# Batch 0's norms pair by pair through Ln and Exp on ScalarE, with its copies and casts moved off ScalarE

## The chip, the cores and the metric

One core of one Trainium2 chip. The metric is the device time of one execution, in microseconds (us), as the median of several. Here "slow" is a run over 1.5% above the fastest of the same kernel. The kernel before has a spread of its own, 475.9 to 483.5 over all its runs (476.21 at a mean clock of 0.999 and 482.3 at 0.987 in one set of rounds), so it is always run beside the kernel that it is compared with. "Clock" is the clock granted to TensorE, the matrix engine, as the profile records it: 1.00 is full speed, 0.50 half.

## The reference

```python
q_n = q / (norm(q, axis=-1) + 1e-6);  k_n likewise          # q, k, v: 8 batches x 12 heads x 448 x 64, fp32
attn = softmax(q_n @ k_n^T / tau)                            # tau = 0.1
x = (attn @ v) laid out as 3584 x 768
h = x @ w_in;  out = (h * sigmoid(1.702 * h)) @ w_out        # 768 -> 2048 -> 768
```

## The kernel before

Two heads make a "pair"; six pairs make a batch. A small planner in the kernel gives each operation an engine, an estimated duration and a due time, and fixes the order on every engine when the program is built. An engine runs its instructions in that order, whatever happens on the chip. Where the plan foresees a gap on TensorE in the first 50 us, it puts filler transposes there, to keep the clock up.

```python
def norm_a(grp):                      # one chain of small VectorE operations for a group of pairs
    ...                               # y = bits of a turned into a first guess of 1/sqrt(a)
    newton(grp, RS_A, RS_B)           # 3 operations
def norm_b(grp):
    newton(grp, 0.5, 1.5)             # 3 operations
    ...                               # y / (y * 1e-6 + 1): add, reciprocal, multiply
groups = [(0,), (1, 2), (3, 4, 5)]    # batch 0: three norms for six pairs

def fill():
    nc.tensor.transpose(out=tps0[:, 2 * S : 2 * S + 128], in_=ident, identity=ident)

# in the plan's emit(): fillers ahead of a TensorE operation that is planned later than TensorE is free
while free < KEEP_WARM and free + FILL_SPARE < now:
    fill()
    free += FILL_US
```

ScalarE squares q and k, VectorE sums, a norm follows, GpSimd scales (VectorE for pair 0's q), TensorE transposes and makes scores, ScalarE takes Exp, TensorE attends. The second part (tanh for the sigmoid) begins with `mm1_h`, line 529 of the kernel before.

## Time and profile before

| | before |
|---|---|
| time, median of 3 (range) | 479.46 us (475.9 to 480.62) |
| span of the profiled run | 479.4 us |
| TensorE busy | 463.7 us, 97% |
| ScalarE busy | 310.0 us, 65% |
| first product of the second part | 42.97 us |
| fillers on TensorE | 326 |

The prediction below shows the lines and reads them. PE is TensorE, PEld its weight loads, DVE VectorE, ACT ScalarE, POOL GpSimd. A line of a timeline gives the start and the time taken in us, engine, line of the kernel, operation, tile written <- tile read with their sizes, how many, and in brackets the wait ahead of it and what ended that. A line of a table of stretches gives the stretch, its length, busy us (and instructions) of the five, the clock, the transfers' share and GB/s. Cuts are marked by "...".

### The profile page before, as it was taken

Reading aid. Unit: us, or ns where it says so; the run is one execution under the profiler, and the core shown is the slowest. Engines: PE = TensorE matmul, PEld = TensorE weight load, DVE = VectorE, ACT = ScalarE, POOL = GpSimd, SP = SyncE. Lnnn points to the kernel's source line nnn. Section 1 sums busy time; section 2 is a strip of 40 time slices with the busy share of each in tenths; the row PEclk is TensorE's granted clock in tenths of the full one; section 3 lists DMA queues with packets and bytes.
Section 4 is the critical chain, followed back from the end, with each engine's and each line's share of the span. In section 5 each row is a group of like instructions: output and inputs, shape, how many; then the busy total and the mean of one; then the engine's idle time right before and its main releaser. Section 6 shows DMA issues by size and latency. Waiting matters only on the chain.

```text
span 479.4 us, 9003 instructions
## 1 busy us (share of the span) xinstructions
PE 463.7 (97%) x3382; PEld 268.0 (56%) x3382; DVE 275.4 (57%) x663; ACT 310.0 (65%) x491; POOL 132.1 (28%) x189
## 2 busy tenths in 40 slices
PE   8889999999999999999999999999999999999996
PEld 8768888664444554445444554445444554555563
DVE  6746887687687736864495735963373315532500
ACT  4669869679887567776777567865666556423411
POOL 1452741656633422406151422415100000000000
PEclk9999999599999999999999999999999999999999
DMA  9999599978965558446564567343310222022022
GB/s 219 238 238 246 89 177 243 261 205 205 231 161 116 140 146 177 115 110 185 145 160 100 140 162 180 95 125 94 89 45 3 62 68 63 2 62 67 1 58 75
DMA packets 81435, 63.50 MB, mean 132 GB/s; under 512 B 40232, under 2 KB 74864, under 8 KB 81392
## 3 DMA queue, kind: packets, MB, share of 16 engines
q1 hardware_dynamic: 77504, 56.41, 47.3%
q0 software_dynamic: 3648, 6.29, 7.3%
q8 instruction: 26, 0.43, 0.4%
q10 hardware_dynamic: 240, 0.23, 0.1%
q14 instruction: 17, 0.14, 0.1%
HBM read 49.81 MB, written 11.14 MB: 127 GB/s over the span
## 4 chain that ended last, share of the span: by engine, by line
PE 75%; DMA 10%; DVE 6%; ACT 4%; SPq 2%; issue 1%; POOL 1%; ACTq 0%
PE mm L554 30%; PE mm L499 22%; PE avp L363 10%; PE sp L344 7%; DMA k<-in_k_dram 4%; DMA w_out<-in_moe_w_out_dram 4%; PE mm L409 2%; ACT expT L355 2%; DVE xT L487 2%; ACT sq L238 1%; DVE n L244 1%; DMA v<-in_v_dram 1%; DMA q<-in_q_dram 1%; DVE gT L516 1%; PE tps L323 1%; SPq L230 1%
## 5 line engine op out<-in xcount | busy, mean ns | idle before, releaser
L355 ACT ACTIVATE expT<-sp 112x896 f16<-112x896 f32 x192 | 166.7, 917 | 57.2 <-PE sp L344 45.9
L554 PE MATMUL mm<-w_out,gT 128*128 128x384 f16 x896 | 155.1, 328 | 0.0
L499 PE MATMUL mm<-xT,w_in 128*128 128x448 f16 x672 | 134.0, 353 | 1.9 <-DVE gT L516 1.9
L554 PEld LDWEIGHTS <-gT 128*128 128x128 f16 x896 | 84.4, 98 | 66.2 <-issue 14.1
L499 PEld LDWEIGHTS <-w_in 128*128 128x128 f16 x672 | 63.2, 98 | 68.5 <-issue 13.5
L516 DVE SCALAR_TENSOR_TENSOR gT<-th,mm 128x448 f16<-128x448 f16 x112 | 67.8, 617 | 56.2 <-ACT th L509 55.7
L509 ACT ACTIVATE th<-mm 128x448 f16<-128x448 f32 x128 | 69.4, 545 | 38.1 <-PE mm L499 31.1
L244 DVE TENSOR_REDUCE n<-sq 112x8 f32<-112x512 f32 x96 | 63.9, 677 | 38.2 <-ACT sq L238 37.7
L307 POOL CAST vt<-v 112x256 f16<-112x256 f32 x84 | 32.3, 402 | 161.9 <-PE avp L363 95.9
L380 DVE TENSOR_SCALAR av<-avp 65x448 f16<-65x448 f32 x72 | 44.4, 617 | 47.2 <-PE avp L363 46.9
L363 PE MATMUL avp<-expT,vt 112*128 112x448 f16 x288 | 66.5, 352 | 0.6 <-DVE av L380 0.6
L295 POOL TENSOR_TENSOR qks<-k,y 112x512 f16<-112x512 f32 x48 | 50.2, 1046 | 56.0 <-DVE y L285 30.9
L565 ACT ACTIVATE ost<-mm 128x384 f32<-128x384 f32 x56 | 27.5, 491 | 44.2 <-PE mm L554 42.6
L295 POOL TENSOR_TENSOR qks<-q,y 112x512 f16<-112x512 f32 x47 | 49.1, 1045 | 6.8 <-DVE xT L487 6.8
L344 PE MATMUL sp<-qkT 64*112 64x448 f16 x288 | 43.0, 372 | 0.0
L363 PEld LDWEIGHTS <-vt 112*128 112x128 f16 x288 | 27.8, 97 | 25.6 <-issue 1.3
L238 ACT ACTIVATE sq<-k 112x512 f32<-112x512 f32 x48 | 30.4, 636 | 14.8 <-DMA k<-in_k_dram 12.9
L487 DVE TENSOR_TENSOR xT<-av,rcb 64x448 f16<-64x448 f16 x72 | 31.3, 434 | 11.8 <-DMA rcb<-rcp 10.8
L238 ACT ACTIVATE sq<-q 112x512 f32<-112x512 f32 x48 | 30.2, 634 | 8.1 <-DMA q<-in_q_dram 5.2
L344 PEld LDWEIGHTS <-qkT 64*112 64x112 f16 x288 | 13.1, 124 | 27.7 <-issue 27.7
L323 PE MATMUL tps<-ident 128*128 128x128 f16 x326 | 23.4, 234 | 4.9 <-DVE qkT L327 3.4
L409 PE MATMUL mm<-vt,expT 112*112 112x65 f16 x384 | 25.7, 222 | 0.5 <-ACT expT L355 0.4
(39 smaller groups left out, 230.3 us busy)
## 6 DMA issues: line engine op xcount, KB each, us to landing
k<-in_k_dram SPq DMA_DIRECT2D x48, 224.0 KB, 3.0
v<-in_v_dram SPq DMA_DIRECT2D x48, 224.0 KB, 3.2
q<-in_q_dram SPq DMA_DIRECT2D x47, 224.0 KB, 4.4
rcb<-rcp SPq DMA_DIRECT2D x24, 168.0 KB, 3.1
w_in<-in_moe_w_in_dram POOLq DMA_DIRECT2D x2, 1536.0 KB, 16.1
w_out<-in_moe_w_out_dram POOLq DMA_DIRECT2D x2, 1536.0 KB, 15.1
out_dram<-ost SPq DMA_DIRECT2D x7, 336.0 KB
out_dram<-ost SPq DMA_DIRECT2D x8, 288.0 KB
```

The costliest lines, as they stand in the source:

```text
L238: return nc.scalar.activation(out=sqs[x, ti], in_=src, func=AF.Square)
L244: nc.vector.tensor_reduce(out=n2s[grp][:, x - grp[0], ti], in_=sqs.pop((x, ti)), axis=AX.X, op=ALU.add,)
L295: return eng.tensor_tensor(out=qkss[x][:, ti].rearrange("p c j d -> p j c d"), in0=src, in1=rss[x][:, ti, :, :, None].to_broadcast((P, 2, ...
L344: nc.tensor.matmul(out=sp[:, j, :S], lhsT=qkT[64 * j : 64 * (j + 1), 1, c * P : (c + 1) * P], rhs=qkT[64 * j : 64 * (j + 1), 0, :], start= ...
L355: nc.scalar.activation(out=e, in_=sps.pop(key)[:, :, :S], func=AF.Exp, scale=inv_tau, **kw)
L363: nc.tensor.matmul(out=ps, lhsT=vts[x % NV][:, c, j], rhs=exps[x, c][:, j], start=(c == 0), stop=(c == C - 1),)
L380: nc.vector.tensor_scalar(out=avs[x][:n, j], in0=ps[:n], scalar1=AV_SCALE, scalar2=None, op0=ALU.mult)
L487: last = nc.vector.tensor_tensor(out=xT[r], in0=av[r, j], in1=rcbs[x // GRP][r, x % GRP], op=ALU.mult)
L499: nc.tensor.matmul(out=ps[:, :S], lhsT=w_in_sb[:, kk, 128 * m : 128 * (m + 1)], rhs=xTs[b, kk], start=(kk == 0), stop=(kk == KT1 - 1),)
L509: nc.scalar.activation(out=ths[key], in_=mms[key][:, :S], func=AF.Tanh, scale=0.851)
L516: nc.vector.scalar_tensor_tensor(out=gts[b // 2][:, m, (b % 2) * S : (b % 2 + 1) * S], in0=ths.pop((b, m)), scalar=1.0, in1=mms.pop((b, m) ...
L554: nc.tensor.matmul(out=mms[b2, t, n][:, :NW], lhsT=gts[b2][:, kk, 128 * t : 128 * (t + 1)], rhs=w_out_sb[:, kk, NW * n : NW * (n + 1)], st ...
```

## The change

The intent: VectorE's Newton chains go. `exp(0.5 * ln(a))` on ScalarE gives the norm, VectorE adds 1e-6 and takes the reciprocal. Each pair of batch 0 has its own norm, so that no pair waits for another's load. To make room on ScalarE, the turned copies go to VectorE and the v casts of pairs 2 to 5 to GpSimd (`XA` and `CA` name the pairs whose copies and casts stay on ScalarE; `SQP`, for squares on GpSimd, is empty).

```diff
+    SQP, SQT, XA, CA = (), (0, 1), (), (0, 1)
...
+    def root(grp):
+        a = n2s[grp]
+        nc.scalar.activation(out=a, in_=a, func=AF.Ln)
+        nc.scalar.activation(out=a, in_=a, func=AF.Exp, scale=0.5)
+
+    def inverse(grp):
+        ...
+        nc.vector.tensor_scalar(out=y, in0=a, scalar1=1e-6, scalar2=None, op0=ALU.add)
+        last = nc.vector.reciprocal(out=y, in_=y)
...
-        copy = nc.scalar.copy if x < HP else nc.gpsimd.tensor_copy
+        copy = nc.scalar.copy if x in CA else nc.gpsimd.tensor_copy
...
-        (nc.scalar.copy if b + h == 0 else nc.vector.tensor_copy)(
+        (nc.scalar.copy if x in XA and not h else nc.vector.tensor_copy)(
...
-    groups = [(0,), (1, 2), (3, 4, 5)]
+    groups = [(x,) for x in range(HP)]
...
+            if first:
+                add(("norm", 0, grp), "ACT", 0.48, early + 0.3, partial(root, grp), after=reds)
+                add(("norm", 1, grp), "DVE", 0.45, early + 0.3, partial(inverse, grp), after=[("norm", 0, grp)])
```

A table load (`ACT_TABLE_LOAD` in the traces) is the instruction that stands on ScalarE wherever it goes over to the functions of another table set.

More of the change, by code (lines that the diff above doesn't have):

```diff
@@ L196 @@
     p_sq = pool("p_sq", 2)
-    p_n = pool("p_n", 2)
+    p_n = pool("p_n", 3)
     p_qks = pool("p_qks", 3)
@@ L233, in load, with sq_pool @@
         )
+    def sq_pool(x, ti):
+        return x in SQP and ti in SQT
     def square(x, ti):
@@ L237, in square @@
         src = (q32, k32)[ti][x]
+        if sq_pool(x, ti):
+            return nc.gpsimd.tensor_tensor(out=sqs[x, ti], in0=src, in1=src, op=ALU.mult)
         return nc.scalar.activation(out=sqs[x, ti], in_=src, func=AF.Square)
@@ L289, in norm_b @@
         return last
+    def root(grp):
[3 more added lines that the diff above has]
+    def inverse(grp):
+        a = n2s.pop(grp)
+        y = p_n.tile([P, len(grp), 2, 2, C], FP32, name=f"yv_{len(grp)}")
+        nc.vector.tensor_scalar(out=y, in0=a, scalar1=1e-6, scalar2=None, op0=ALU.add)
+        last = nc.vector.reciprocal(out=y, in_=y)
+        for x in grp:
+            rss[x] = y[:, x - grp[0]]
+        return last
     def scale(x, ti, eng):
@@ L623 @@
                 takes=[(nm, 1)], dma=PAIR, hold=hold, turn=True)
-            add(("sq", ti, x), "ACT", 0.53, early + ti * 0.1, partial(square, x, ti),
-                after=[("load", nm, x)], takes=[("sq", 1)])
+            pl = sq_pool(x, ti)
+            add(("sq", ti, x), "POOL" if pl else "ACT", 1.0 if pl else 0.53, early + ti * 0.1, partial(square, x, ti),
+                after=[("load", nm, x)], takes=[("sq", 1), ("port", int(pl))], frees=[("port", int(pl))])
             add(("red", ti, x), "DVE", 0.6, early + 0.2, partial(reduce, x, ti),
@@ L634 @@
             n = len(grp)
+            if first:
+                add(("norm", 0, grp), "ACT", 0.48, early + 0.3, partial(root, grp), after=reds)
+                add(("norm", 1, grp), "DVE", 0.45, early + 0.3, partial(inverse, grp), after=[("norm", 0, grp)])
+        if x == grp[0] and not first:
             add(("norm", 0, grp), "DVE", 0.78 + 0.06 * n, early + 0.3, partial(norm_a, grp), after=reds, **port)
@@ L638 @@
             takes=[("v", 1)], dma=PAIR, hold=hold, turn=True)
-        add(("cast", x), "ACT" if first else "POOL", 0.64 if first else 0.75, s - 0.5, partial(cast_v, x),
-            after=[("load", "v", x)], takes=[("vt", 1), ("port", 1 - first)], frees=[("v", 1), ("port", 1 - first)])
+        ca = x in CA
+        add(("cast", x), "ACT" if ca else "POOL", 0.64 if ca else 0.75, s - 0.5, partial(cast_v, x),
+            after=[("load", "v", x)], takes=[("vt", 1), ("port", 1 - ca)], frees=[("v", 1), ("port", 1 - ca)])
         if x < TURN:
@@ L664 @@
                     frees=[("xs", 1)])
-                add(("x", x, h), "ACT" if first and not h else "DVE", 0.35, sh + 1, partial(turned_h, x, h), after=[("turn", x, h)],
+                add(("x", x, h), "ACT" if x in XA and not h else "DVE", 0.35, sh + 1, partial(turned_h, x, h), after=[("turn", x, h)],
                     takes=[("x", 1 - h)], frees=[("mm", 1)])
```

## The prediction

> **What bounds the kernel now.** I read the busy table first, then the forty slices, the table of stretches, the chain of waits, and last the timelines of ScalarE, GpSimd, VectorE and TensorE over the first 60 us, because the change touches batch 0 alone (pairs 0 to 5).
>
> ```profile
> PE 463.7 (97%) x3382; PEld 268.0 (56%) x3382; DVE 275.4 (57%) x663; ACT 310.0 (65%) x491; POOL 132.1 (28%) x189
> ...
> PE   8889999999999999999999999999999999999996
> ...
> ACT  4669869679887567776777567865666556423411
> ...
> PEclk9999999599999999999999999999999999999999
> ...
> PE mm L554 30%; PE mm L499 22%; PE avp L363 10%; PE sp L344 7%; DMA k<-in_k_dram 4%; DMA w_out<-in_moe_w_out_dram 4%; PE mm L409 2%; ACT expT L355 2%; DVE xT L487 2%; ACT sq L238 1%; DVE n L244 1%; DMA v<-in_v_dram 1%; DMA q<-in_q_dram 1%; DVE gT L516 1%; PE tps L323 1%; SPq L230 1%
> ...
> 0.00:10.00 10.00, 8.64 (x109) 8.64 (x110) 6.67 (x39) 3.77 (x6) 1.32 (x7) 1.00 0.88 212
> 10.00:20.00 10.00, 9.21 (x162) 8.73 (x159) 7.67 (x21) 7.43 (x16) 4.42 (x6) 1.00 1.13 247
> 20.00:30.00 10.00, 7.90 (x127) 6.74 (x125) 5.31 (x18) 6.35 (x13) 5.21 (x6) 1.00 1.11 218
> 30.00:40.00 10.00, 8.48 (x128) 6.94 (x127) 3.73 (x10) 7.64 (x12) 2.71 (x3) 1.00 1.12 270
> 40.00:50.00 10.00, 9.78 (x140) 8.63 (x139) 9.09 (x28) 9.94 (x17) 4.54 (x8) 1.00 0.72 180
> ...
> 70.00:100.00 30.00, 27.94 (x300) 22.78 (x298) 21.42 (x57) 22.50 (x36) 10.40 (x18) 0.83 1.02 245
> ...
> 1.36 10.82 PE L323 MATMUL tps<-ident 128*128 128x128 f16 x145 [1.36 <-POOL ident masks.py:199]
> ...
> 42.97 1.32 PE L529 MATMUL mm<-xT,w_in 128*128 128x224 f16 x12
> ...
> 1.19 1.28 ACT L238 ACT_TABLE_LOAD   x1 [1.19 <-PEq L807]
> ...
> 14.66 0.92 ACT L355 ACTIVATE expT<-sp 112x896 f16<-112x896 f32 x1 [2.19 <-PE sp L392]
> ...
> 17.00 0.82 POOL L590 DMA_DIRECT2D w_in<-in_moe_w_in_dram  x1 [2.70 <-DVE y L285]
> ...
> 26.67 1.04 POOL L295 TENSOR_TENSOR qks<-k,y 112x512 f16<-112x512 f32 x1 [4.79 <-DVE y L285]
> ```
>
> See first that TensorE is busy in nearly every slice, so from about 43 us on the span is its work laid end to end. Ahead of that, "busy" deceives: 145 of the first instructions are filler transposes of the identity that keep its clock up. The first useful product of the second part (the 12 matmuls at 42.97) marks when the filling ends. So the start is a latency chain (load, square, sum, norm, scale, transpose, scores, exponential, attend), and a microsecond saved or lost before that mark is a microsecond of span, if the TensorE work behind it is unchanged. ScalarE is far from full at first (3.8 us of the first 10) but 9.9 of 10 between 40 and 50. The granted clock fell to half for part of one slice near 85 us; the whole 70 to 100 stretch has 0.83, which is 5.1 us of full clock lost, about the spread of the three runs (475.9 to 480.62).
>
> The last two lines show what the change aims at. GpSimd stood idle 2.7 and 4.8 us for a Newton result: pairs 1 and 2 share one norm, and so do pairs 3 to 5, so pair 3 cannot be scaled before pair 5 is loaded. Their scales start only at 17.84 and 26.67.
>
> **What the Trainium skill says.** "ScalarE: Activation LUTs", section "What ACT_TABLE_LOAD costs", gives 1283 ns for a table load plus about 1380 ns of drain, 2.66 us for a switch; the same section gives an activation with immediates 186 ns + 0.833 ns an element. The trace agrees with the load (1.28) and the activation (917 ns for 896 elements in the row of exponentials; the formula says 932), but its one load is followed by a wait for a transfer, so it cannot show the drain. "Table sets: the hidden batching unit" on that page says that Exp sits with tanh in one set, and that Ln and Exp together have another set of their own. "ScalarE activation tables: per-element evaluation and per-set limits", section "Table sets in the compiler and the runtime", says that the back end places loads by the longest run. Here the order of the built instructions decides: the kernel before has 1 load, the changed one 13. Every Ln is preceded by a load of another set, and every Exp of a norm by a load of the first set. The shared set is not used. "TensorE: Matmul & The Clock Gate", section "What's actually happening", says that an idle window of about 3.4 us halves the clock; the 5 in the clock row, just after TensorE's waits of 1.25, 0.41 and 0.41 us at 84 us, fits.
>
> **The change part by part.**
> Removed from VectorE: three Newton chains of 10 small operations. Pair 0's runs from 6.44 to 8.57, 2.1 us; that of pairs 1 and 2 from 14.34 to 16.69, 2.3 us; that of pairs 3 to 5 is 2.5 us of operations about a qkT copy. Sum 6.9 us. Added: six times an addition and a reciprocal on 16 columns (0.21 + 0.29 from their start spacing), 3.0 us, and six turned copies at about 0.2, 1.2 us. Net relief about 2.7 us on an engine that is not the bound here.
> Removed from ScalarE: six turned copies at 0.24 spacing, 1.4 us, and four pairs of v casts at 0.6, 2.4 us. Added: six Ln and six Exp on 16 columns, an estimate of 0.2 us each by the page's formula, 2.4 us; and 12 table loads at 1.28, 15.4 us. Net +14 us, before any drain. ScalarE worked 25.2 us in the first 40, so about 39 of 40 is asked of it.
> GpSimd gains the four v casts (0.74 a pair, 3.0 us), lying beside other work. Its first weight load moves behind pair 1's two scales, but pair 1 no longer waits for the second weight load. The fillers ahead of pair 0's transposes drop from 145 to 127, at 75 ns 1.3 us less.
>
> Now the chain, placing the new ScalarE order with the old spacings (square 0.52, exponential 0.82, casts 0.6, load 1.28; the ends of the last one where something depends on it).
> Pair 0: squares as before, done 6.47; load 7.75; Ln 8.0; load 9.3; Exp 9.5. Inverse on VectorE until 10.0, then its scale until 10.7 and GpSimd's until 11.8, against 8.6, 9.3 and 10.4. Nearly free, since the transposes began only at 12.02, behind fillers.
> Pair 1: squares to 10.55, load, Ln, load, Exp: 13.6. The copy of pair 0's transposes stands behind this inverse on VectorE: 14.1 instead of 12.61. Scores at 14.7 instead of 14.22. GpSimd scales pair 1 at 14.1, 3.7 us earlier than before.
> Pair 2: two squares and a v cast to 15.25, norm to 18.3. Only then comes a square and the first softmax exponential, at 18.7 instead of 14.66.
> Pair 3: norm 19.6 to 22.6, then a square and the second exponential at 23.0 instead of 16.51. Both score buffers are held until then, so TensorE waits.
> Pair 4: two squares, a v cast and a square to 25.65, norm to 28.7. Two exponentials, a square, two exponentials: 32.5. Pair 5: norm to 35.5. Inverse 36.1, GpSimd scales to 38.1, transposes, copy, scores: its two exponentials end near 43.2 after those of pairs 3, 4 and 0 again. Attend, normalise, turn: the first product at about 46.0 against 42.97, 3.0 late. Useful TensorE work ahead of it is alike (seven attends, some eight halves of scores in both).
> Each of the 12 switches lies on this serial chain, so 0.1 us of hand-over at each adds 1.2: 4.2 us late. Behind the mark, ScalarE has no squares of batch 1 done where before it had four, so five tanh steps later it needs 8 exponentials, 10 squares and 5 tanh (13.9 us) where the trace took 13.4. Another 0.5 to 2 us lost; I take 1.3. After that ScalarE is some 75% busy and TensorE hides it. TensorE's gaps between 17 and 37 us get longer, two of them near 2.5 us with few fillers between: I allow 1.5 us for a halved clock there. Sum 4.2 + 1.3 + 1.5 = 7.0 us: 486.5 us.
>
> **The rivals.**
> One: the switch costs the page's full 2.66 us. Nothing in the old trace excludes it. For it: the page says so. Against: a drain of about the load's own length could be the sequencer waiting for the same load and not a further cost; the other page gives only 1283 ns between sets. It would add 12 x 1.38 = 16.6 us to the chain, longer clock gaps too: about 500 to 505 us. I give it one in four.
> Two: what the change intends. Loads hide in ScalarE's early idle time and pair-by-pair norms free GpSimd sooner: pairs 3 to 5 start up to 4 us earlier than the old 26.67. For it: ScalarE has 15 idle us in the first 40 and the scales of pair 3 should come at 22.9. Against: the exponentials that pairs 0 and 1 need are queued behind the loads. If a few more of the loads lie in waits than I placed there, 476 to 480 us.
> Three: the half-clock spell of 82 to 92 us does not recur in the new order: up to 5.1 us gained, which would bring my sum back to about 481; or a second one falls on useful work: 491.
>
> **Range and chances.** Between rival two and a mild form of rival one lie 8 chances in 10: 478.5 to 501 us. Faster by over 2% is below 469.9, for which the mark would have to come by 34 us while ScalarE is full: 3%. Slower by over 2% is above 489.05: rival one (25%), half of the cases with an intermediate hand-over (8%), and a bad clock spell (5%): 38%. Within 2%: 59%.
>
> **What would show each step.** Thirteen table loads with the gap behind each to its Ln or Exp: under 0.2 us speaks for my sum, over 1 us for rival one. First exponential at 18 to 20 us; the second over 3.5 us later. First product at 45.5 to 48. ScalarE over 90% in the stretches from 10 to 40. Scales of pairs 1 and 3 at about 14 and 23, earlier than before, yet without gain. The clock row with a new 5 in the first four slices. I am wrong if the loads overlap with waits and the mark comes before 43, or if the span changes by much more than the mark does: then the rest of the order, not ScalarE's start, decides.

## The result

The changed kernel takes 491.95 us (median of 4, 491.48 to 492.33) against 479.55 (the three runs above and one more): a ratio of 1.0273, 95% interval 1.0227 to 1.032, slower. (Ratios here are the mean time of one kernel's fast runs over that of the other's of the same rounds, so not quite the ratio of the medians.)

The changed kernel's page: the busy row, then TensorE, ScalarE and the granted clock in the forty slices.

```profile
PE 471.2 (96%) x3315; PEld 273.3 (56%) x3315; DVE 272.6 (56%) x651; ACT 322.9 (66%) x501; POOL 135.3 (28%) x197
...
PE   8769999999999999999999999999999999999996
...
ACT  7994768699888755876678656784677456423411
...
PEclk9575789999999999999999999999999999999999
```

ScalarE gained 12.9 us of work, and the clock row has changed: five of the first six slices are below 9. Cut along the clock, the table of stretches of the changed kernel says it better.

```profile
13.90:24.20 10.30, 8.76 (x79) 7.64 (x79) 4.55 (x11) 10.18 (x17) 6.67 (x7) 0.50 1.03 195
24.20:31.00 6.80, 4.06 (x70) 3.63 (x69) 3.46 (x10) 6.74 (x12) 2.81 (x4) 1.00 1.11 211
31.00:54.90 23.90, 22.54 (x197) 18.20 (x195) 8.40 (x26) 14.73 (x19) 6.07 (x13) 0.50 0.78 199
...
68.50:72.00 3.50, 3.50 (x26) 2.92 (x25) 1.45 (x5) 1.06 (x2) 3.50 (x8) 0.51 0.21 14
```

From 13.9 to 31 us ScalarE works nearly without a break (10.18 of 10.30, 6.74 of 6.80) and TensorE waits for it (4.06 of 6.80 busy). Then the clock falls to half for 23.9 us, and now TensorE is full, at half speed, and ScalarE waits (14.73 of 23.90).

The changed kernel's ScalarE in order of time, pair 0's norm and the later exponentials:

```profile
5.75 0.63 ACT L244 ACTIVATE sq<-k 112x512 f32<-112x512 f32 x1 [0.23 <-DVE n L250]
6.40 1.28 ACT L300 ACT_TABLE_LOAD   x1
7.70 0.21 ACT L300 ACTIVATE n<-n 112x16 f32<-112x16 f32 x1
7.93 1.28 ACT L301 ACT_TABLE_LOAD   x1
9.22 0.21 ACT L301 ACTIVATE n<-n 112x16 f32<-112x16 f32 x1
9.35 0.61 ACT L244 ACTIVATE sq<-q 112x512 f32<-112x512 f32 x1
...
18.66 0.90 ACT L376 ACTIVATE expT<-sp 112x896 f16<-112x896 f32 x1
...
23.03 0.90 ACT L376 ACTIVATE expT<-sp 112x896 f16<-112x896 f32 x1
...
35.64 0.21 ACT L301 ACTIVATE n<-n 112x16 f32<-112x16 f32 x1
35.77 2.52 ACT L376 ACTIVATE expT<-sp 112x896 f16<-112x896 f32 x3
41.07 1.77 ACT L376 ACTIVATE expT<-sp 112x896 f16<-112x896 f32 x2 [2.79 <-PE sp L413]
```

A norm is load, Ln, load, Exp, 3.0 us, and the step from one to the next costs 0.01 to 0.02 us: there is no drain behind a load. From 4.4 to 38 us nothing on this engine waits long; from then on it does, for scores.

The changed kernel's TensorE where it waited, and where the clock was down:

```profile
29.49 0.40 PE L413 MATMUL sp<-qkT 64*112 64x224 f16 x4 [2.19 <-ACT expT L376]
...
42.33 1.67 PE L430 MATMUL mm<-vt,expT 112*112 112x65 f16 x16
...
51.09 2.45 PE L550 MATMUL mm<-xT,w_in 128*128 128x224 f16 x12
...
55.58 0.98 PE L430 MATMUL mm<-vt,expT 112*112 112x65 f16 x16
```

Sixteen attend matmuls take 1.67 us in the spell and 0.98 after it. The first product of the second part, called the mark from here on, comes at 51.09, 8.1 us later than before.

### The profile page after: what moved, and what is told of

Read it like the earlier page. It is cut to its first block, busy times and chain, and to the rows that moved or that the text cites. A ratio compares the mean times of both kernels' runs of the same rounds, so it can differ in the third digit from the quotient of the medians.

```text
span 489.7 us, 8871 instructions
## 1 busy us (share of the span) xinstructions
PE 471.2 (96%) x3315; PEld 273.3 (56%) x3315; DVE 272.6 (56%) x651; ACT 322.9 (66%) x501; POOL 135.3 (28%) x197
## 4 chain that ended last, share of the span: by engine, by line
PE 75%; ACT 8%; DVE 6%; DMA 6%; SPq 2%; issue 2%; POOL 0%; ACTq 0%; DVEq 0%
PE mm L575 27%; PE mm L520 22%; PE avp L384 9%; PE sp L365 6%; PE mm L550 4%; DMA k<-in_k_dram 3%; PE mm L430 3%; DMA q<-in_q_dram 2%; ACT sq L244 2%; ACT expT L376 2%; PE sp L413 2%; ACT L300 2%; DVE n L250 1%; ACT L301 1%; DVE gT L537 1%
## 5 line engine op out<-in xcount | busy, mean ns | idle before, releaser
L575 PEld LDWEIGHTS <-gT 128*128 128x128 f16 x896 | 83.6, 98 | 65.6 <-issue 13.9
L328 POOL CAST vt<-v 112x256 f16<-112x256 f32 x92 | 35.5, 406 | 161.1 <-PE avp L384 93.0
L316 POOL TENSOR_TENSOR qks<-k,y 112x512 f16<-112x512 f32 x42 | 44.0, 1047 | 48.0 <-DVE y L291 32.8
L316 POOL TENSOR_TENSOR qks<-q,y 112x512 f16<-112x512 f32 x42 | 44.0, 1047 | 5.2 <-DVE xT L508 5.2
L384 PEld LDWEIGHTS <-vt 112*128 112x128 f16 x288 | 27.9, 97 | 24.6 <-issue 0.2
L430 PE MATMUL mm<-vt,expT 112*112 112x65 f16 x384 | 27.0, 231 | 0.1
```

Source lines behind the costliest of these rows:

```text
L316: return eng.tensor_tensor(out=qkss[x][:, ti].rearrange("p c j d -> p j c d"), in0=src, in1=rss[x][:, ti, :, :, None].to_broadcast((P, 2, ...
L384: nc.tensor.matmul(out=ps, lhsT=vts[x % NV][:, c, j], rhs=exps[x, c][:, j], start=(c == 0), stop=(c == C - 1),)
L430: nc.tensor.matmul(out=ps[:P, o : o + D + 1], lhsT=exps[x, h, c // 2][:, j, at : at + P], rhs=vts[x % NV][:, c, j, 63 * j : 63 * j + D + 1 ...
L575: nc.tensor.matmul(out=mms[b2, t, n][:, :NW], lhsT=gts[b2][:, kk, 128 * t : 128 * (t + 1)], rhs=w_out_sb[:, kk, NW * n : NW * (n + 1)], st ...
```

## The experiments

Theory A: the 12 table loads lie end to end on ScalarE's chain, and the plan, which reckons 0.48 us for a norm of 3.0, did not order the work or the fillers for them. Theory B: the halved clock is the larger cost and has its own remedy. Theory C: the pair-by-pair order, or the moved copies and casts, do the harm. All outputs are right.

**One table set for Ln and Exp.** The order on every engine is that of the changed kernel; 2 loads are left of 13, the second ahead of the first tanh.

```diff
+        if (x, ti) == (0, 1):
+            nc.scalar.preload_act_table_set("natural_log_exp_and_others")
```

> The changed kernel with one table load at the start that names the set holding both Ln and Exp; the order of all other instructions on every engine is unchanged, and 2 loads are left of 13. Theory A (the 12 switches are the cause, alone or by what they make TensorE's clock do): the 14 us of loads leave ScalarE's chain, the first product comes at 36 to 41 us instead of 51.1, and the time is 470 to 477 us, below the kernel before. Rival (the pair-by-pair order, or the casts and copies moved to GpSimd and VectorE, cost the time): it stays at 485 us or more.

473.86 us, ratio 0.9917 (0.9849 to 0.9985). Its first exponential, the end of pair 5's norm, its second load and its first product, in the timelines of ScalarE and TensorE:

```profile
13.07 0.90 ACT L378 ACTIVATE expT<-sp 112x896 f16<-112x896 f32 x1
...
23.70 0.21 ACT L303 ACTIVATE n<-n 112x16 f32<-112x16 f32 x1
...
37.23 1.28 ACT L532 ACT_TABLE_LOAD   x1
...
34.43 1.32 PE L552 MATMUL mm<-xT,w_in 128*128 128x224 f16 x12
```

Same order, same casts and copies, same pairing: theory C falls, and in this order the loads with all they cause are worth 18.1 us of median (491.95 - 473.86, two sets of rounds). The mark came even before the 36 to 41 us of the expectation.

**Pairing alone, with Newton steps.**

```diff
-    groups = [(0,), (1, 2), (3, 4, 5)]
+    groups = [(x,) for x in range(HP)]        # in the kernel before; its small pool with 3 buffers
```

> The kernel before with its norms of batch 0 taken pair by pair, still by Newton steps on VectorE: no Ln, no loads, casts and copies where they were. It shows the worth of the pairing alone. If pairing alone frees GpSimd early enough: 474 to 478 us. If the six Newton chains (12.6 us of VectorE in place of 6.9) take it back: 479 to 484 us. If the pairing is what made the change slow: over 488 us.

480.76 us, ratio 1.0055 (0.9996 to 1.0113). Pairing alone is worth nothing with ten VectorE operations a pair; nor is it what made the change slow.

**More fillers at two waits.**

```diff
+            for _ in range({("s", 2, 0, 0): 28, ("s", 4, 0, 0): 14}.get(names[i], 0)):
+                fill()
```

> The changed kernel with 28 and 14 more filler transposes in front of the scores of pairs 2 and 4, where TensorE sat idle 2.2 and 1.2 us; nothing else moves. If the half clock from 31 to 55 us is a cost of its own, set off by the idle time: the clock row shows no 5 there, the first product comes at 45.5 to 47.5 us and the time is 485 to 488 us. If the clock is only a symptom and ScalarE would hold TensorE back anyway: product at 50 to 52, time 490 to 493 us.

Inconclusive. Four runs gave 490.98, 481.9, 486.98 and 487.68 us, at mean clocks of 0.972, 0.989, 0.979 and 0.971; the ratio over the fast runs is 1.0157 (1.0061 to 1.0253), and the profiled run was slow. In it the spells moved instead of going: half clock from 14.3 to 17.7, 24.6 to 31.4 and 38.2 to 55.3, and the first product at 52.64. The same program thus spread over 9 us with the clock that it was granted, which speaks for a cost of its own, but the run at 481.9 has no trace and stays unexplained: the next kernel but one, at full clock, never came that low.

**The plan told the true time of a norm.**

```diff
-                add(("norm", 0, grp), "ACT", 0.48, early + 0.3, partial(root, grp), after=reds)
+                add(("norm", 0, grp), "ACT", 3.06, early + 0.3, partial(root, grp), after=reds)
```

> The changed kernel with its plan told 3.06 us for a norm on ScalarE in place of 0.48; the loads stay, but the plan orders the work around them and puts 483 fillers instead of 259. If the harm is partly that the plan did not know of the loads: 482 to 487 us. If only the loads on ScalarE's chain count: 488 to 493 us.

480.9 us, ratio 1.0058 (0.999 to 1.0125): 11 us better than the change with one number altered, and all 13 loads still there. The first product is no earlier (50.81), but batch 1's squares and other work have been drawn ahead of it and the clock holds. A later mark is not a later end when more has been done ahead of it; the Newton kernel, with its mark at 47.27, shows the same.

**The clock held, order unchanged.** Eleven waits get 210 more fillers, and the early ones a PSUM tile of their own.

```diff
+MORE = {("tp", 0): 10, ("s", 0, 0, 0): 24, ("s", 1, 0, 0): 36, ("at", 0, 0): 40, ("s", 2, 0, 0): 34, ("s", 4, 0, 0): 22}
+MORE |= {("at", 3, 0): 8, ("tp", 5): 10, ("at", 4, 0): 8, ("s", 5, 0, 0): 6, ("at", 5, 0): 12}
...
+        to = tps0[:, 2 * S : 2 * S + 128] if (2, 0) in avps or xTs else warm[:, :64].bitcast(FP16)
```

> The changed kernel with all its table loads and the same order of all other instructions, but 210 more filler transposes in eleven waits of TensorE, and a PSUM tile of their own for the early ones, so that they need not wait for VectorE's copies. If the clock is the larger part of the loss: a mean clock of 0.985 or more, the first product at 45 to 48 us and 480 to 485 us. If ScalarE's chain alone makes the loss: clock up, but still 488 us or more.

487.26 us, ratio 1.0161 (1.0101 to 1.022). Its stretches, the end of pair 5's norm on ScalarE, its first product and the fillers behind it:

```profile
20.00:30.00 10.00, 8.85 (x142) 7.90 (x142) 4.06 (x12) 9.90 (x16) 4.29 (x6) 1.00 1.11 204
30.00:40.00 10.00, 8.64 (x144) 7.62 (x143) 4.33 (x14) 8.08 (x11) 6.44 (x12) 1.00 1.11 270
40.00:50.00 10.00, 9.46 (x143) 8.10 (x142) 3.85 (x13) 6.26 (x8) 0.75 (x2) 1.00 0.84 235
...
35.51 0.22 ACT L307 ACTIVATE n<-n 112x16 f32<-112x16 f32 x1
...
47.93 1.31 PE L559 MATMUL mm<-xT,w_in 128*128 128x224 f16 x12
...
57.00 0.72 PE L353 MATMUL tps<-ident 128*128 128x128 f16 x10
...
58.03 1.07 PE L353 MATMUL tps<-ident 128*128 128x128 f16 x16
...
59.37 1.07 PE L353 MATMUL tps<-ident 128*128 128x128 f16 x16
```

Full clock throughout, ScalarE as full as in the changed kernel, and the mark at 47.93 in place of 51.09. The time lies between the two outcomes that I had set: holding the clock is worth 4.7 us of median (5.4 by the ratios, 1.0273 - 1.0161 of 479.6, each ratio known to about half a per cent).

That is net of what the added fillers cost themselves. From the end of pair 5's norm to the mark it is 15.2 us in the changed kernel (35.85 to 51.09), 12.2 here (35.73 to 47.93) and 10.5 in the one-set kernel (23.91 to 34.43), which is at full clock there too. From the next scores (36.58 here, 24.89 there) to the mark TensorE runs 63 fillers here and 19 there, and is idle for 0.5 to 0.6 us in both. So the fillers took back some 1.7 us. My estimate from these numbers is that the clock alone cost about 7 us (5.4 + 1.7), half of the loss, and that the chain alone makes the mark about 3.3 us late (47.93 - 1.7 - 42.97).

What is left at full clock, 7.7 us by the ratio, splits in two, as book-keeping between two orders: 5.0 us in the mark (47.93 - 42.97, the fillers' 1.7 among them), the other 2.7 behind it. There stand 42 fillers in three blocks, 2.9 us of TensorE, where the kernel before has one block of 6. That the plan had nothing ready from batch 1 to put there is likely, and was not tested.

Against the one-set kernel of the same order (0.9881 in its longer measurement below) the full-clock kernel differs by 0.028 of 478.5 us, 13.4 us, again with the fillers' 1.7. Pair 5's norm ends 11.8 us later in it, and the 12 loads more that it has ahead of that are 12 x 1.283 = 15.4 us. About three quarters of the loads' time lies on the chain; in the one-set kernel ScalarE stands waiting for VectorE and for transfers in part of the room that they left.

**The loads alone, in the kernel before.** An Ln and an Exp on a scratch tile of ones, six times, for which nothing waits; the plan again reckons 0.48.

```diff
+        if first:
+            add(("lut", x), "ACT", 0.48, due_of(x) - 3.7, partial(switch, x), after=[("red", ti, x) for ti in range(2)])
```

> The kernel before, with six times an Ln and an Exp on a scratch tile of 16 ones on ScalarE, for which nothing waits: the 12 table loads and nothing else of the change. If the loads cost by the room they take on ScalarE in front of squares and exponentials: 485 to 492 us, most of the change's loss. If the loads hide in ScalarE's idle time and it is the norm that waits for them that costs: 479 to 482 us.

495.52 us, ratio 1.0335 (1.028 to 1.039), worse than the change itself and above both expectations. The table of stretches shows the same picture:

```profile
20.00:30.00 10.00, 6.56 (x70) 6.14 (x72) 4.67 (x12) 9.88 (x18) 3.13 (x4) 0.75 1.12 224
30.00:40.00 10.00, 8.13 (x78) 6.93 (x75) 2.61 (x9) 8.89 (x17) 6.05 (x6) 0.50 1.12 256
40.00:50.00 10.00, 8.57 (x81) 6.84 (x80) 3.09 (x7) 3.38 (x5) 0.00 (x0) 0.50 0.77 186
```

The loads do not hide in ScalarE's idle time, not even when nothing waits for their result, because what stands behind them on the engine does wait. How much of it is the clock, and how much the plan that reckons 0.48, was not taken apart here.

**Copies and casts back on ScalarE, with one set.**

```diff
-    SQP, SQT, XA, CA = (), (0, 1), (), (0, 1)
+    SQP, SQT, XA, CA = (), (0, 1), range(6), range(6)
```

> The one-set kernel with the turned copies and all six v casts of batch 0 back on ScalarE as before: what the second part of the change is worth. If ScalarE is the bound in batch 0: 1.5 to 4 us slower than the one-set kernel's 473.9. If transfers bound the start instead: within 1 us of it.

475.64 us, ratio 0.9913 (0.9841 to 0.9985) against 473.86 and 0.9917 in other rounds. The ratios agree, so moving copies and casts is worth nothing that these runs resolve.

**The kernel before without fillers.**

```diff
-WARM_FROM, KEEP_WARM, FILL_US, FILL_SPARE = 1.5, 50.0, 0.056, 0.3
+WARM_FROM, KEEP_WARM, FILL_US, FILL_SPARE = 1.5, 0.0, 0.056, 0.3
```

> The kernel before without any filler transposes; it shows the worth of TensorE's clock in the start by itself. If a halved clock in the start costs what I now put on it: clock 0.95 to 0.97 and 484 to 492 us. If the start waits for the other engines whatever the clock: 478 to 481 us.

483.16 us, ratio 1.0082 (1.0017 to 1.0146): between the two expectations. Two lines of it contradict one another, a stretch and a group of attends in it:

```profile
30.00:40.00 10.00, 9.40 (x84) 7.19 (x80) 3.15 (x7) 6.82 (x10) 0.52 (x1) 1.00 1.12 287
...
31.88 1.71 PE L409 MATMUL mm<-vt,expT 112*112 112x65 f16 x16
```

The clock column says 1.00, the sixteen attends take 1.71 us where they take 0.98 at full clock. The trace's clock record begins at 48.8 us, and ahead of it the column shows its default. Half clock up to there, without the fillers' own time, costs 4 us in all (1 to 7 by the interval), and the mark is 2.0 us later (45.00): before the mark, much of TensorE's work has slack.

**The one-set kernel again.** No edit.

> The one-set kernel once more, in five rounds, to settle a gain of under 1%. If the gain over the kernel before is real: a ratio of 0.985 to 0.995 with the interval below 1. If the first three rounds flattered it: the interval reaches 1.

472.53 us in 6 runs against 478.41, ratio 0.9881 (0.9848 to 0.9913). It beats both kernels.

**One set under the told plan.** Both edits of the first and of the told kernel.

> The kernel whose plan was told 3.06 us for a norm, with the one table set in place of the 12 loads: its order and its 483 fillers kept, the loads gone. If that order hides the loads (ScalarE waits there for other engines): within 2 us of the 480.9 with the loads. If the loads still lengthen the chain under that order: 473 to 477 us.

481.64 us, ratio 1.0065 (1.0034 to 1.0097), as with the loads (1.0058). TensorE's fillers and its first product in the two, the group of fillers first from the told kernel with loads, then without:

```profile
L344 PE MATMUL tps<-ident 128*128 128x128 f16 x483 | 31.3, 227 | 4.7 <-DVE qkT L348 3.3 <-POOL ident masks.py:199 1.4
...
50.81 1.32 PE L550 MATMUL mm<-xT,w_in 128*128 128x224 f16 x12
```

```profile
L346 PE MATMUL tps<-ident 128*128 128x128 f16 x483 | 31.0, 227 | 4.7 <-DVE qkT L350 3.3 <-POOL ident masks.py:199 1.4
...
50.58 1.31 PE L552 MATMUL mm<-xT,w_in 128*128 128x224 f16 x12
```

Taking the loads out moves the mark by 0.2 us: the 483 fillers and the order that were planned around the loads now set TensorE's pace (from 20 to 30 us it is busy 9.44 us with the loads and 9.43 without, ScalarE 9.88 and 4.65). So these two do not say what a load costs in itself; they say that time planned as waiting is spent whether the wait comes or not. By how much the told order would gain with fewer fillers stays open.

## Why the prediction was right or wrong

The range (478.5 to 501) held 491.95. The side did not: 59% were on "within 2%", 38% on slower. The sum of 7.0 us was to be about 13.1 (0.0273 of 479.6). In part it is luck that the range held: its upper end was set for a mild form of rival one, which fell, and the distance was filled by the clock, to whose bad case the prediction gave 5%.

1. **Thirteen loads, all in series on ScalarE: right.** The placing by old spacings held within half a microsecond: first exponential 18.7, measured 18.66; second 23.0, measured 23.03; end of pair 5's norm 35.5, measured 35.85. The one-set kernel shows that they are the cause. Of the signs, the scales of pairs 1 and 3 came at 14.11 and 23.41, as foretold and without gain; ScalarE over 90% held from 10 to 30 us, not from 30 to 40 (7.92 of 10).
2. **Mark 4.2 us late: close for the chain, wrong for the kernel.** The changed kernel has it 8.1 late, the full-clock kernel 5.0, and the chain alone about 3.3 by the estimate above. The hand-over of 0.1 us at each switch, 1.2 in the sum, was not there (0.01 to 0.02). The path from pair 5's norm to the mark, reckoned at 10.5 us, is 10.5 in the one-set kernel at full clock and 15.2 in the changed kernel, most of it at half clock.
3. **Behind the mark, 1.3 us: too small.** It was about 2.7. I counted ScalarE's work and not the 42 fillers that I had the means to count in the built order. The one-set kernel has them too: in its second measurement the mark is 9.7 us earlier than before (33.25) and the time 5.7, so 4.0 are lost behind it, its load ahead of the first tanh (1.28) among them.
4. **The clock, 1.5 us: the term most mis-sized.** 4.7 to 5.4 us net of the fillers that held it, about 7 by the estimate above. I foresaw gaps of 2.5 us with few fillers, and reckoned a short spell. It was 37.7 us at half clock in three spells, the longest of them over the stretch in which TensorE had caught up with ScalarE and had no slack left. The reading that it rested on was off as well: the waits of 1.25, 0.41 and 0.41 us ahead of the old spell make 2.1 us and do not fit an idle window of 3.4, and the record has that spell at 85.2 to 95.5 us, not 82 to 92.
5. **Rival one, a switch of 2.66 us: fell**, by the 0.02 us behind each load. The kernel is slow without it.
6. **Rival two, the intended gain: fell for this kernel**, but the gain exists once the loads go: 1.2% in the one-set kernel. Whether the norm's price or the pairing brings it was not taken apart; the Newton kernel shows only that pairing by itself does not.
7. **Rival three: half right.** The spell of the kernel before at 85 us did not come back; others came earlier and fell on useful work, the case for which it had 491 us.

## What to carry to other kernels

A function outside the loaded table set costs 1.3 us at each change, in series with all that its engine does next; count the loads in the built program, and name one set that holds both functions if there is one. Where a planner fixes the order, a wrong duration in it is a cost of its own: after altering one number the same kernel with the same loads lost 11 us less. And a TensorE that waits in its start may pay a second time, at half clock, when it no longer waits.

## What the Trainium skill lacked or had wrong

- "ScalarE: Activation LUTs", section "What ACT_TABLE_LOAD costs": a switch is given as 1283 ns plus 1380 ns of drain. The load is right (1.28 us, all 13), the drain isn't there: behind each of the 12 loads of the norms the next activation starts after 0.01 to 0.02 us, 1.3 us in all for a switch.
- The same page, section "Table sets: the hidden batching unit", has Ln then Exp as one load. This build made two for each, 12 for six norms, until the set with both was named; then 2 in the whole program, and 491.95 became 473.86 us. No page says how a kernel names a set. "Longest run" in "ScalarE activation tables: per-element evaluation and per-set limits", section "Table sets in the compiler and the runtime", isn't what placed these loads.
- "TensorE: Matmul & The Clock Gate", section "What's actually happening", has an idle window of about 3.4 us halve the clock and a busy one release it. Here no wait was longer than 2.2 us, and in the 3.4 us ahead of the three spells TensorE was busy 1.4, 1.5 and 2.5 us; the longest spell then lasted 23.9 us with TensorE busy 22.5 of them. What sets the clock here stays open.
- "TensorE: Matmul & The Clock Gate", section "Seeing it yourself", warns that clock events in a trace are unreliable, but no page says that the record begins with the first change to full clock and that what lies ahead of it reads as 1.00. In the changed kernel it begins at 7.1 us, and fillers stand 107 ns apart ahead of that and 56 behind it; without fillers it began at 48.8 us, and matmuls under a column of 1.00 took 1.7 times their time (1.71 against 0.98 us for sixteen attends).
